# Windowed attention with a folded feed-forward on one core: another written order for steps 0 to 7, and five feed-forward slices between values and scores from step 8 on

## The chip, the cores and the metric

The kernel runs on one core of one Trainium2 chip. The metric is device time in microseconds (us). The engines are PE (TensorE), DVE (VectorE), ACT (ScalarE), POOL (GpSimd) and SP (SyncE), which here issues every transfer.

## The reference

Attention over 4 batches x 8 heads x 768 positions x 64, with a key kept if it is one of the first 8 or among the last 96, a bias that falls with distance, a softmax, and then a feed-forward part on all 3072 tokens:

```python
scores = scale * np.matmul(q, k.transpose(0, 1, 3, 2))
scores = np.where(keep, scores + bias[None, :, :, :], -1000000000.0)
scores = scores - np.max(scores, axis=-1, keepdims=True)
a = np.exp(scores)
a = a / (np.sum(a, axis=-1, keepdims=True) + 1e-09)
x = np.matmul(a, v)            # then 4 x 768 tokens of 512 numbers
a = x @ w1                     # w1, w2: 512 x 1024, float64
b = x @ w2
h = a * b @ w3                 # w3: 1024 x 1024, float64
return h @ w_out               # w_out: 1024 x 512, float64
```

## The kernel before, in words

**Attention** goes in 24 steps of 128 queries (all 8 heads, 6 steps to a batch). A step s has these parts, named as in the written order: `S.s`, the scores (64 small matmuls, L487); `R.s.q`, scores plus bias and their maxima, for four groups q of 32 queries (DVE, L496); `E.s.q`, the exponentials (ACT, L503); `s.s`, the sums and their reciprocals (DVE, L508 and L509); `c.s`, the scaling (ACT, L518, in steps 0 to 4, DVE, L521, after that); `X.s.0` and `X.s.1`, two transposes (DVE, L526); `V.s`, the values (128 small matmuls, 80 in the first step of a batch, L539); `h.s` and `l.s`, which copy the result out as a high and a low half (ACT L562, DVE L567). Scores and values go to one tile of PSUM, `sc`: in each of its four banks the values take the first 128 columns and the scores those behind. A step's keys and queries (`d.q<s>`) and values (`d.v<s>`) are loaded into two buffers each, so step s+2 loads what step s has left.

**The weights** come as float64 and are turned into float32 by DVE, in three instructions of 512 columns for each of 40 pieces: `A`, `B` and `C` (L143, L145, L147) of `t` (16 half blocks of w3), `o` (8 blocks of w_out) and `w` (16 blocks of w1 and w2). `d.x` loads a piece into one of eight landing buffers (L123), which is free again after the `C` of the piece before; w4 to w15 use only four of them. w3 and w_out are multiplied once: `F.f.k` is one of 64 fold matmuls (L167, each in two passes), `ph`/`pl` split the product, `wh`/`wl` split w1 and w2 (ACT and DVE).

**The feed-forward** goes in six units of 512 tokens, four steps each. A unit has 48 slices of six matmuls of 512 columns: 32 of the first product (`U.f.n.half`, L192 to L194) and 16 of the second (`Z.t.j`, L220 to L222). After the second slice of each f ACT copies out the gate `a` (L198), after the fourth DVE multiplies (`g`, L202), and `gh` and `gl` (L207, L212) split it.

**Order.** Steps 0 to 7, all weight work and unit 0 are issued from one hand-written list, `ORDER`: PE, DVE, ACT and SP each run their own part of it in that sequence. From step 8 on a loop sets the order of PE and ACT; DVE and SP follow a planner, which decides in advance by estimated times. Before the change a step's loop runs one slice after each of its four q groups, then half of `SLICES[s]`, then sums, scaling and transposes, the other half, the values, at once the scores of the next step, and only then `high(s)` and `low(s)`. `SLICES` is 4 for step 8 and 8 for the later ones.

Of the kernel before, what the change touches and what calls it, by code (L numbers as in the profile page):

```python
# [18 lines left out]
B, H, S, D = 4, 8, 768, 64  # L19
# [11 lines left out]
R = 32  # L31
# [5 lines left out]
NB = S // P  # L37
# [7 lines left out]
ORDER = """
d.t30 nt d.t00 d.q0 A.t30 B.t30 d.t20 bias d.o1 S.0 d.o0 A.t00 B.t00 C.t00 d.q2 C.t30 A.o1 B.o1 d.t41 A.o0 B.o0 d.t01 C.o0 C.o1 F.0.0 d.o2 A.t20 B.t20
d.o5 R.0.0 F.3.0 R.0.1 E.0.0 R.0.2 d.t31 E.0.1 R.0.3 A.t01 E.0.2 F.0.1 A.o2 d.v0 B.o2 E.0.3 F.3.1 d.t60 A.o5 B.t01 s.0 d.o4 C.t20 c.0 C.t01 F.2.0 d.o6
A.t31 B.o5 F.2.1 C.o2 d.t10 X.0.0 F.0.2 d.t11 X.0.1 F.3.2 A.o6 V.0 d.q1 B.o6 C.o6 F.2.2 A.t10 A.o4 d.o3 B.t10 h.0 l.0 C.t10 S.1 C.o5 B.t31 A.o3 F.1.0
d.q3 C.t31 R.1.0 F.1.1 R.1.1 E.1.0 R.1.2 F.1.2 E.1.1 R.1.3 B.o3 S.2 E.1.2 C.o3 E.1.3 B.o4 F.0.3 d.q4 s.1 C.o4 F.1.3 c.1 F.0.4 d.t51 F.3.3 d.t50 F.0.5
X.1.0 F.3.4 X.1.1 d.v1 A.t11 F.0.6 R.2.0 d.w4 F.3.5 R.2.1 E.2.0 A.t50 F.2.3 d.t21 E.2.1 B.t50 V.1 C.t50 d.v2 R.2.2 R.2.3 E.2.2 d.o7 A.t51 S.3 B.t11  # L50
E.2.3 C.t11 d.v3 h.1 F.3.6 l.1 d.w7 s.2 F.1.4 c.2 A.o7 B.o7 F.1.5 C.o7 F.1.6 B.t51 d.w14 F.0.7 X.2.0 F.1.7 d.t40 A.t21 ph.0 X.2.1 F.3.7 ph.1 pl.0 V.2
pl.1 ph.3 B.t21 C.t21 A.t40 F.2.4 d.t71 h.2 C.t51 l.2 F.5.0 d.w0 pl.3 F.2.5 B.t40 C.t40 F.5.1 A.t71 d.t70 F.2.6 B.t71 A.w0 F.5.2 C.t71 F.2.7 B.w0 d.w5
C.w0 F.5.3 ph.2 A.t70 d.w2 wh.0 F.4.0 pl.2 B.t70 F.5.4 C.t70 F.4.1 A.t41 d.w1 B.t41 F.7.0 C.t41 F.5.5 A.w2 B.w2 F.7.1 C.w2 F.5.6 A.w1 wh.2 F.7.2 B.w1
C.w1 F.5.7 wl.2 wh.1 F.7.3 R.3.0 ph.5 F.4.2 R.3.1 E.3.0 pl.5 F.7.4 E.3.1 R.3.2 F.4.3 R.3.3 E.3.2 wl.1 S.4 E.3.3 A.w5 B.w5 F.7.5 s.3 C.w5 c.3 F.4.4
A.t60 d.w11 B.t60 F.7.6 C.t60 d.w3 F.4.5 wl.0 wh.5 X.3.0 F.6.0 d.v4 X.3.1 F.7.7 d.t61 A.w4 F.6.1 ph.7 A.w3 V.3 B.w3 pl.7 C.w3 R.4.0 wh.3 F.6.2 A.t61
d.v5 E.4.0 wl.3 F.4.6 h.3 A.w7 l.3 F.6.3 B.w7 U.0.0.0 C.w7 B.t61 wh.7 d.w13 F.4.7 C.t61 U.0.0.1 R.4.1 ph.4 E.4.1 pl.4 F.6.4 wl.7 A.w11 U.0.1.0 R.4.2
R.4.3 E.4.2 F.6.5 B.w11 E.4.3 C.w11 U.0.1.1 s.4 wh.11 d.w6 B.w4 c.4 F.6.6 C.w4 U.1.0.0 wl.11 d.w8 wl.5 F.6.7 wh.4 X.4.0 U.1.0.1 ph.6 X.4.1 a.0 pl.6
V.4 a.1 g.0 A.w6 gh.0 B.w6 U.1.1.0 C.w6 gl.0 wh.6 d.w9 wl.6 U.1.1.1 wl.4 A.w8 U.2.0.0 g.1 A.w9 gh.1 B.w9 U.2.0.1 gl.1 B.w8 U.2.1.0 a.2 C.w8 C.w9 wh.8
d.w12 wh.9 U.2.1.1 wl.8 d.w15 wl.9 U.3.0.0 g.2 d.q6 A.w13 gh.2 A.w12 U.3.0.1 B.w12 d.q5 A.w15 C.w12 U.3.1.0 a.3 B.w15 d.w10 wh.12 C.w15 U.3.1.1 B.w13
wh.15 C.w13 S.5 g.3 wh.13 A.w10 gh.3 B.w10 U.4.0.0 C.w10 gl.2 wh.10 U.4.0.1 wl.10 A.w14 U.4.1.0 a.4 B.w14 C.w14 gl.3 wh.14 U.4.1.1 R.5.0 R.5.1 E.5.0  # L60
U.5.0.0 g.4 E.5.1 R.5.2 R.5.3 gh.4 U.5.0.1 E.5.2 gl.4 wl.13 S.6 E.5.3 wl.12 a.5 s.5 U.5.1.0 c.5 X.5.0 U.5.1.1 X.5.1 U.6.0.0 g.5 R.6.0 gh.5 R.6.1 E.6.0
U.6.0.1 gl.5 R.6.2 E.6.1 R.6.3 U.6.1.0 a.6 wl.15 E.6.2 wl.14 h.4 U.6.1.1 E.6.3 l.4 V.5 g.6 s.6 gh.6 c.6 U.7.0.0 h.5 d.v7 gl.6 l.5 X.6.0 d.v6 Z.0.0
d.q7 X.6.1 U.7.0.1 d.q8 Z.0.1 a.7 U.7.1.0 Z.0.2 U.7.1.1 V.6 g.7 gh.7 gl.7 S.7 h.6 Z.0.3 R.7.0 R.7.1 E.7.0 R.7.2 Z.1.0 ot.0 R.7.3 E.7.1 l.6 S.8 E.7.2
E.7.3 Z.1.1 s.7 c.7 Z.1.2 X.7.0 Z.1.3 X.7.1 V.7 ot.1 Z.2.0 h.7 l.7 Z.2.1 Z.2.2 Z.2.3 Z.3.0 ot.2 Z.3.1 Z.3.2 Z.3.3 ot.3
"""
W = 2 * T
SLOPES = [2.0 ** -(h + 1) for h in range(H)]
# [324 lines left out]
def banded(ctx, tc, ff, ns, nt, nf, oki, ident, qk, vx):  # L392
# [273 lines left out]
```

## Time and profile before

| what | value |
|---|---|
| median of 3 runs | 579.94 us (579.9 to 583.39) |
| the profiled execution | 583.23 us, its span 581.4 us |
| mean granted TensorE clock | 0.984 of full speed |
| PE busy | 534.8 us, 92% |
| DVE busy | 275.5 us, 47% |
| ACT busy | 196.5 us, 34% |

A busy PE is not PE at its peak, since matmuls are pipelined and the record of one covers parts of its neighbours. So what PE can lose is read from the distance of its starts, and from the stretches in which nothing starts. The profiled execution is 3.29 us longer than the median.

### The profile page before, as it was taken

What the parts mean: (1) busy time and instruction counts of PE and PEld (TensorE: products, weight loads), DVE (VectorE), ACT (ScalarE), POOL (GpSimd) and SP (SyncE); (2) the same over time, 40 slices, a digit from 0 to 9 for tenths busy, and PEclk for the clock granted to TensorE, in tenths of its full rate; (3) what the DMA queues carried; (4) which work ended last, traced back from release to release, by engine and by line L of the source; (5) the groups of instructions that cost most, each with busy time, mean ns of one, the idle gap of its engine ahead of it and who ended that gap; (6) DMA issues with size and microseconds to landing.
All of it is one profiled execution on the core that took longest, in us unless ns stands there. A gap on an engine that the chain in (4) does not pass through costs nothing.

```text
span 581.4 us, 14382 instructions
## 1 busy us (share of the span) xinstructions
PE 534.8 (92%) x6272; PEld 411.3 (71%) x6272; DVE 275.5 (47%) x779; ACT 196.5 (34%) x609; POOL 4.0 (1%) x26
## 2 busy tenths in 40 slices
PE   1776999989999999999999989999999999999995
PEld 0343445767778787788878778888877788888884
DVE  5874898989642445324534413544243454012200
ACT  4342334635432344323423331433234243122210
POOL 2000000000000000000000000000000000000000
PEclk9888899999999999999999989999999999999999
DMA  8958445361342112213220330222132000100011
GB/s 296 348 178 348 151 139 183 114 219 48 127 158 92 50 39 76 73 45 120 88 77 12 108 112 19 74 89 75 53 124 89 8 30 20 38 18 1 0 38 41
DMA packets 17879, 56.98 MB, mean 98 GB/s; under 512 B 1936, under 2 KB 3984, under 8 KB 17808
## 3 DMA queue, kind: packets, MB, share of 16 engines
q1 hardware_dynamic: 17808, 55.98, 27.7%
q8 instruction: 51, 0.84, 0.6%
q14 instruction: 20, 0.16, 0.1%
HBM read 49.68 MB, written 6.29 MB: 96 GB/s over the span
## 4 chain that ended last, share of the span: by engine, by line
PE 75%; DMA 10%; DVE 9%; issue 3%; ACT 1%; SPq 0%; ACTq 0%
PE m L192 13%; PE m L193 13%; PE m L194 13%; PE o L220 8%; PE o L221 7%; PE o L222 7%; PE sc L539 6%; PE sc L487 5%; PE w L167 2%; DMA stage<-w 2%; DMA raws<-w_out 2%; DMA more_raws<-w 1%; DMA qr<-qk 1%; DMA vr<-vx 1%; DVE t3s L147 1%
## 5 line engine op out<-in xcount | busy, mean ns | idle before, releaser
L503 ACT ACTIVATE pr<-pr,mx 128x136 f32<-128x136 f32 (+2 forms) x192 | 74.5, 390 | 31.7 <-DVE mx L496 31.7
L202 DVE TENSOR_TENSOR g<-m,a 128x512 f32<-128x512 f32 x48 | 33.1, 689 | 101.6 <-PE m L194 101.2
L192 PE MATMUL m<-xh,w1h 128*128 128x512 f32 x192 | 77.3, 402 | 0.4 <-ACT xh L562 0.4
L220 PE MATMUL o<-wh,gh 128*128 128x512 f32 x192 | 76.7, 400 | 0.0
L192 PE MATMUL m<-xh,w2h 128*128 128x512 f32 x192 | 75.7, 394 | 0.0
L221 PE MATMUL o<-wl,gh 128*128 128x512 f32 x192 | 75.5, 393 | 0.0
L222 PE MATMUL o<-wh,gl 128*128 128x512 f32 x192 | 75.3, 392 | 0.0
L193 PE MATMUL m<-xl,w1h 128*128 128x512 f32 x192 | 75.0, 391 | 0.2 <-DVE xl L567 0.2
L194 PE MATMUL m<-xh,w1l 128*128 128x512 f32 x192 | 74.8, 390 | 0.0
L194 PE MATMUL m<-xh,w2l 128*128 128x512 f32 x192 | 74.7, 389 | 0.0
L193 PE MATMUL m<-xl,w2h 128*128 128x512 f32 x192 | 74.7, 389 | 0.0
L167 PE MATMUL w<-wo,t 128*128 128x512 f32 x128 | 64.9, 655 | 7.3 <-DVE wo L147 4.3
L207 ACT ACTIVATE gh<-g 128x512 fp32r<-128x512 f32 x48 | 30.3, 631 | 115.5 <-DVE g L202 115.5
L487 PE MATMUL sc<-qr 64*32 64x136 f32 (+3 forms) x1536 | 33.3, 288 | 30.7 <-DMA qr<-qk 14.9
L567 DVE TENSOR_TENSOR xl<-sc,xh 128x512 fp32r<-128x512 f32 x24 | 16.6, 691 | 82.6 <-ACT xh L562 82.5
L167 PEld LDWEIGHTS w<-wo,t 128*128 128x128 f32 x128 | 26.0, 211 | 38.6 <-issue 26.4
L487 PEld LDWEIGHTS sc<-qr 64*32 64x32 f32 x1536 | 23.1, 111 | 37.9 <-issue 16.6
L539 PEld LDWEIGHTS sc<-pt,vr 32*64 32x64 f32 x2880 | 38.5, 130 | 11.9 <-issue 6.7
L198 ACT ACTIVATE a<-m 128x512 f32<-128x512 f32 x48 | 28.5, 594 | 51.4 <-PE m L194 51.2
L212 DVE TENSOR_TENSOR gl<-g,gh 128x512 fp32r<-128x512 f32 x48 | 33.1, 690 | 22.6 <-ACT gh L207 22.3
L192 PEld LDWEIGHTS m<-xh,w1h 128*128 128x128 f32 x192 | 36.0, 188 | 11.0 <-issue 2.4
L220 PEld LDWEIGHTS o<-wh,gh 128*128 128x128 f32 x192 | 36.4, 189 | 9.3 <-issue 1.9
(85 smaller groups left out, 619.1 us busy)
## 6 DMA issues: line engine op xcount, KB each, us to landing
qr<-qk SPq DMA_DIRECT2D x20, 720.0 KB, 5.6
vr<-vx SPq DMA_DIRECT2D x20, 512.0 KB, 4.0
out_dram<-ot SPq DMA_DIRECT2D x24, 256.0 KB, 2.0
stage<-w3t SPq DMA_DIRECT2D x9, 512.0 KB, 5.2
raws<-w SPq DMA_DIRECT2D x6, 512.0 KB, 4.0
more_raws<-w SPq DMA_DIRECT2D x6, 512.0 KB, 3.6
more_raws<-w_out SPq DMA_DIRECT2D x5, 512.0 KB, 8.5
qr<-qk SPq DMA_DIRECT2D x4, 528.0 KB, 5.3
```

The costliest lines, as they stand in the source:

```text
L167: self.nc.tensor.matmul(self.prod[f], lhsT=self.t3[f, z][:, i * P:(i + 1) * P].bitcast(F32), rhs=self.wo[:, k].bitcast(F32), start=k == 0, ...
L192: self.nc.tensor.matmul(ps, lhsT=mh, rhs=xh[:, i], start=i == 0, stop=False)
L193: self.nc.tensor.matmul(ps, lhsT=mh, rhs=xl[:, i], start=False, stop=False)
L194: self.nc.tensor.matmul(ps, lhsT=ml, rhs=xh[:, i], start=False, stop=i == NCC - 1)
L202: self.nc.vector.tensor_tensor(out=self.g[f], in0=self.ps[f, 1], in1=self.a[f], op=ALU.mult)
L212: self.nc.vector.tensor_tensor(out=self.gl[:, f], in0=self.g[f], in1=self.gh[:, f].bitcast(F32), op=ALU.subtract)
L220: self.nc.tensor.matmul(ps, lhsT=self.gh[:, f, ts], rhs=ff.wh[:, f], start=f == 0, stop=False)
L221: self.nc.tensor.matmul(ps, lhsT=self.gh[:, f, ts], rhs=ff.wl[:, f], start=False, stop=False)
L222: self.nc.tensor.matmul(ps, lhsT=self.gl[:, f, ts], rhs=ff.wh[:, f], start=False, stop=f == NFC - 1)
L487: nc.tensor.matmul(sc[hp * R:(hp + 1) * R, i, cols], lhsT=m[rows, hp, KW + q * R:KW + (q + 1) * R], rhs=m[rows, hp, k0 + w0:k0 + w1], star ...
L503: nc.scalar.activation(x, x, AF.Exp, bias=mx[:, q, u:u + 1], scale=-1.0, accum_out=sm[:, q, u:u + 1])
L539: nc.tensor.matmul(sc[cols, hp, q0 * R:q1 * R], lhsT=v[rows, i, cols], rhs=pt[rows, u, i, q0 * R:q1 * R], start=n == 0, stop=n == len(bloc ...
```

## The change

`SLICES` goes. In the loop from step 8 on the split is fixed: one slice after each q group, none before the sums, three between the transposes and the values, then `high(s)` and `low(s)`, then five slices, then the scores of the next step. A step has 12 slices in both kernels, but step 8, which had 8 and now has 12.

`ORDER` is replaced by another sequence of the same 504 entries. The size check is now loaded first, followed by w3's blocks t10, t11 and t31 and by w_out's o1, o4, o2 and o3; the first fold is of row 1; scores and values stand mostly apart from each other on PE; w15 is loaded early and unpacked last of all.

```diff
-SLICES = [4] * 9 + [8] * (B * NB - 9)
 ORDER = """
-d.t30 nt d.t00 d.q0 A.t30 B.t30 d.t20 bias d.o1 S.0 d.o0 A.t00 B.t00 C.t00 d.q2 C.t30 A.o1 B.o1 d.t41 A.o0 B.o0 d.t01 C.o0 C.o1 F.0.0 d.o2 A.t20 B.t20
...
+nt d.t10 d.t11 d.t31 bias d.o1 A.t10 B.t10 d.o4 A.t11 C.t10 d.o2 B.t11 C.t11 d.o3 A.t31 A.o1 B.t31 d.q0 C.t31 A.o4 d.o0 B.o1 A.o2 B.o2 d.t20 C.o1 C.o2
+d.q1 A.o3 S.0 B.o3 C.o3 d.t00 A.o0 B.o0 d.t30 C.o0 R.0.0 F.1.0 d.q2 R.0.1 E.0.0 R.0.2 E.0.1 F.1.1 R.0.3 A.t20 E.0.2 S.1 d.v0 A.t00 B.t00 E.0.3 d.o6
+C.t00 F.1.2 s.0 d.t50 A.t30 c.0 F.0.0 B.t30 F.1.3 d.t01 B.t20 C.t20 F.0.1 d.v1 C.t30 F.2.0 X.0.0 F.0.2 d.q3 X.0.1 F.3.0 A.o6 B.o6 V.0 d.w15 A.t01 C.o6
+R.1.0 d.o5 F.0.3 R.1.1 E.1.0 R.1.2 F.3.1 d.t70 h.0 R.1.3 E.1.1 F.2.1 B.t01 E.1.2 S.2 C.t01 l.0 E.1.3 B.o4 F.3.2 d.q4 s.1 A.o5 c.1 F.2.2 B.o5 C.o4
+F.3.3 d.o7 C.o5 F.1.4 d.t71 X.1.0 F.0.4 X.1.1 F.1.5 d.t41 R.2.0 V.1 R.2.1 E.2.0 d.w2 R.2.2 E.2.1 A.o7 B.o7 F.1.6 h.1 C.o7 E.2.2 F.0.5 l.1 R.2.3 F.1.7
+E.2.3 S.3 A.w2 ph.1 B.w2 F.0.6 C.w2 d.q5 s.2 wh.2 pl.1 F.3.4 c.2 A.t50 F.0.7 d.t60 B.t50 F.3.5 C.t50 d.t21 wl.2 F.2.3 ph.0 X.2.0 F.3.6 d.t40 pl.0
+F.5.0 X.2.1 d.v2 F.3.7 R.3.0 R.3.1 E.3.0 F.5.1 R.3.2 ph.3 A.t21 F.5.2 E.3.1 B.t21 F.5.3 C.t21 E.3.2 A.t40 F.2.4 R.3.3 A.t70 E.3.3 S.4 A.t41 B.t41
+C.t41 V.2 d.q6 s.3 B.t40 c.3 d.t51 C.t40 F.2.5 A.t60 B.t60 d.w4 F.4.0 B.t70 h.2 F.2.6 X.3.0 F.4.1 X.3.1 F.2.7 l.2 A.t51 F.4.2 ph.2 A.t71 pl.3 F.4.3
...
+X.4.1 U.0.0.0 ph.4 R.5.0 pl.4 E.5.0 V.4 R.5.1 R.5.2 E.5.1 R.5.3 E.5.2 wl.4 S.6 C.t61 E.5.3 wl.5 U.0.0.1 s.5 A.w9 B.w9 F.6.4 C.w9 U.0.1.0 c.5 wh.9 d.w7
...
+U.2.1.1 C.w8 B.w10 wh.8 d.w11 U.3.0.0 g.2 C.w10 gh.2 wh.10 d.w14 U.3.0.1 gl.2 wl.10 wl.8 U.3.1.0 a.3 A.w12 B.w12 U.3.1.1 C.w12 A.w14 wh.12 d.w13 B.w14
+U.4.0.0 g.3 C.w14 gh.3 U.4.0.1 A.w11 wh.14 gl.3 wl.12 U.4.1.0 a.4 A.w13 B.w11 C.w11 U.4.1.1 B.w13 wh.11 C.w13 U.5.0.0 g.4 wh.13 gh.4 wl.13 U.5.0.1
+gl.4 wl.11 a.5 U.5.1.0 A.w15 B.w15 C.w15 U.5.1.1 wl.14 wh.15 wl.15 U.6.0.0 g.5 h.4 gh.5 l.4 U.6.0.1 gl.5 V.5 a.6 U.6.1.0 X.6.0 h.5 d.v7 l.5 d.q8 X.6.1
+Z.0.0 R.7.0 R.7.1 E.7.0 U.6.1.1 R.7.2 E.7.1 R.7.3 Z.0.1 g.6 E.7.2 U.7.0.0 gh.6 E.7.3 gl.6 S.8 s.7 c.7 Z.0.2 U.7.0.1 V.6 a.7 U.7.1.0 X.7.0 h.6 l.6
+U.7.1.1 X.7.1 V.7 g.7 gh.7 gl.7 Z.0.3 h.7 l.7 Z.1.0 ot.0 Z.1.1 Z.1.2 Z.1.3 Z.2.0 ot.1 Z.2.1 Z.2.2 Z.2.3 Z.3.0 ot.2 Z.3.1 Z.3.2 Z.3.3 ot.3
 """
...
                     slices(1)
-                slices(SLICES[s] // 2)
                 sums(s)
                 scale(s, nc.vector)
                 turn(s, 0)
                 turn(s, 1)
-                slices(SLICES[s] - SLICES[s] // 2)
+                slices(3)
                 values(s)
+                high(s)
+                low(s)
+                slices(5)
                 if s + 1 < n:
                     scores(s + 1)
-                high(s)
-                low(s)
             slices(10 ** 6)
```

## Rows read from the trace of the kernel before

**Rows 1.** The page, its first part: busy time, share of the span and instructions of PE and DVE.

```profile
PE 534.8 (92%) x6272; PEld 411.3 (71%) x6272; DVE 275.5 (47%) x779; ACT 196.5 (34%) x609; POOL 4.0 (1%) x26
```

**Rows 2.** Busy time by stretches: the stretch, its length, each engine's busy time and instructions, the granted clock, the DMA engines' share, GB/s.

```profile
0.00:62.00 62.00, 38.05 (x513) 19.20 (x514) 40.52 (x119) 25.13 (x91) 3.97 (x26) 0.89 0.74 275
62.00:99.00 37.00, 35.64 (x390) 16.89 (x389) 32.11 (x74) 13.97 (x41) 0.00 (x0) 1.00 0.54 184
99.00:151.00 52.00, 47.72 (x434) 36.43 (x434) 46.40 (x115) 27.01 (x80) 0.00 (x0) 1.00 0.31 107
...
187.00:504.00 317.00, 306.55 (x4038) 251.00 (x4036) 129.60 (x399) 106.27 (x343) 0.00 (x0) 0.99 0.20 65
```

**Rows 3.** The instructions of PE in order of time around the end of the written order (start, duration, engine, line, tiles, shape).

```profile
186.32 0.39 PE L192 MATMUL m<-xh,w1h 128*128 128x512 f32 x1
```

**Rows 4.** All that PE waited for from 187 to 505 us: total, times, longest.

```profile
PE sc L487 <- issue: 10.4, 9, 1.6
```

**Rows 5.** PE in order of time from the last slice before V.9 to the first after S.10; in brackets the idle time before an instruction and what ended it.

```profile
217.73 0.39 PE L194 MATMUL m<-xh,w2l 128*128 128x512 f32 x1
218.05 1.81 PE L539 MATMUL sc<-pt,vr 32*64 32x128 f32 x128
219.79 0.69 PE L487 MATMUL sc<-qr 64*32 64x136 f32 x31
221.81 0.74 PE L487 MATMUL sc<-qr 64*32 64x136 f32 x33 [1.33 <-issue]
222.47 0.50 PE L192 MATMUL m<-xh,w1h 128*128 128x512 f32 x1
222.82 0.40 PE L193 MATMUL m<-xl,w1h 128*128 128x512 f32 x1
```

**Rows 6.** The page, its third part: the queue that carries instructions (packets, MB, share).

```profile
q8 instruction: 51, 0.84, 0.6%
```

**Rows 7.** The chain of waits from step 8 to step 23: start, length, what. V.8, the gap in S.16 and a slice behind it, V.16 with S.17 and V.17, and V.23.

```profile
197.36 1.74 PE sc L539 x87
...
341.90 1.60 issue
...
345.03 0.43 PE o L221
...
362.52 1.74 PE sc L539 x88
364.26 1.13 PE sc L487 x64
...
381.94 1.74 PE sc L539 x87
...
502.38 1.74 PE sc L539 x88
```

**Rows 8.** Busy time by stretches, the one behind the gap in S.16 (columns as in rows 2).

```profile
344.00:347.00 3.00, 3.00 (x27) 2.21 (x11) 1.94 (x14) 1.60 (x6) 0.00 (x0) 0.57 0.61 178
```

**Rows 9.** DVE in order of time in step 10, from the product of its fourth slice to its transposes.

```profile
228.29 0.69 DVE L202 TENSOR_TENSOR g<-m,a 128x512 f32<-128x512 f32 x1 [0.17 <-PE m L194]
...
229.12 1.29 DVE L521 TENSOR_TENSOR pr<-pr,sm 128x1088 f32<-128x1088 f32 x1
230.33 0.69 DVE L212 TENSOR_TENSOR gl<-g,gh 128x512 fp32r<-128x512 f32 x1
230.94 1.56 DVE L526 STREAM_TRANSPOSE pt<-pr 128x640 f32<-128x640 f32 x2
```

**Rows 10.** ACT in order of time in step 10: the gate that stands between the second and the third of its four groups of exponentials.

```profile
225.77 0.58 ACT L198 ACTIVATE a<-m 128x512 f32<-128x512 f32 x1
```

**Rows 11.** The chain of waits from 95 to 152 us: the pace of one matmul of a slice and of one fold (two passes).

```profile
100.56 0.23 PE m L192
...
101.25 0.86 PE w L167 x2
```

**Rows 12.** Groups of DVE instructions by line in 0 to 200 us (count, busy time, mean ns of one, idle time before): the first and the third instruction of an unpacking.

```profile
L147 DVE SCALAR_TENSOR_TENSOR t<-stage,t 128x512 int32<-128x512 int32 x9 | 6.2, 689 | 0.2
...
L143 DVE TENSOR_SCALAR t<-stage 128x512 int32<-128x512 int32 x9 | 3.8, 424 | 1.0 <-DMA stage<-w3t 1.0
```

**Rows 13.** The loads of weight pieces (L123) in 0 to 187 us: who waited for their landing (us, times), and the time from issue to landing.

```profile
  DVE t L143: 8.3, 5
  DVE t3s L143: 5.2, 8
  DVE wo L143: 4.8, 4
...
DMA to landing us min/median/max: 3.4/5.1/12.7
```

**Rows 14.** SP in order of time: the issue of q3 and q4, after 6.5 us in which SP issued nothing.

```profile
36.39 4.69 SPq L458 DMA_DIRECT2D qr<-qk  x2
```

**Rows 15.** Busy time by stretches, 10 to 15 us (columns as in rows 2).

```profile
10.00:15.00 5.00, 0.99 (x43) 0.50 (x31) 3.22 (x6) 4.84 (x15) 0.25 (x2) 1.00 1.02 408
```

**Rows 16.** PE in order of time in the first 62 us: S.0, the first folds, and the second part of S.3.

```profile
9.51 1.48 PE L487 MATMUL sc<-qr 64*32 64x40 f32 x64 [9.51 <-DMA qr<-qk]
15.24 6.13 PE L167 MATMUL w<-wo,t 128*128 128x512 f32 x8 [4.26 <-DVE wo L147]
...
56.15 1.15 PE L487 MATMUL sc<-qr 64*32 64x136 f32 x29 [3.30 <-issue]
```

More of the change, by code (lines that the diff above doesn't have):

```diff
@@ L43 @@
 FIRST = 5
-SLICES = [4] * 9 + [8] * (B * NB - 9)
 ORDER = """
-d.t30 nt d.t00 d.q0 A.t30 B.t30 d.t20 bias d.o1 S.0 d.o0 A.t00 B.t00 C.t00 d.q2 C.t30 A.o1 B.o1 d.t41 A.o0 B.o0 d.t01 C.o0 C.o1 F.0.0 d.o2 A.t20 B.t20
-d.o5 R.0.0 F.3.0 R.0.1 E.0.0 R.0.2 d.t31 E.0.1 R.0.3 A.t01 E.0.2 F.0.1 A.o2 d.v0 B.o2 E.0.3 F.3.1 d.t60 A.o5 B.t01 s.0 d.o4 C.t20 c.0 C.t01 F.2.0 d.o6
-A.t31 B.o5 F.2.1 C.o2 d.t10 X.0.0 F.0.2 d.t11 X.0.1 F.3.2 A.o6 V.0 d.q1 B.o6 C.o6 F.2.2 A.t10 A.o4 d.o3 B.t10 h.0 l.0 C.t10 S.1 C.o5 B.t31 A.o3 F.1.0
@@ L49 @@
[L49 to L64, printed above, removed]
+nt d.t10 d.t11 d.t31 bias d.o1 A.t10 B.t10 d.o4 A.t11 C.t10 d.o2 B.t11 C.t11 d.o3 A.t31 A.o1 B.t31 d.q0 C.t31 A.o4 d.o0 B.o1 A.o2 B.o2 d.t20 C.o1 C.o2
@@ new lines @@
+E.2.3 S.3 A.w2 ph.1 B.w2 F.0.6 C.w2 d.q5 s.2 wh.2 pl.1 F.3.4 c.2 A.t50 F.0.7 d.t60 B.t50 F.3.5 C.t50 d.t21 wl.2 F.2.3 ph.0 X.2.0 F.3.6 d.t40 pl.0
+F.5.0 X.2.1 d.v2 F.3.7 R.3.0 R.3.1 E.3.0 F.5.1 R.3.2 ph.3 A.t21 F.5.2 E.3.1 B.t21 F.5.3 C.t21 E.3.2 A.t40 F.2.4 R.3.3 A.t70 E.3.3 S.4 A.t41 B.t41
+C.t41 V.2 d.q6 s.3 B.t40 c.3 d.t51 C.t40 F.2.5 A.t60 B.t60 d.w4 F.4.0 B.t70 h.2 F.2.6 X.3.0 F.4.1 X.3.1 F.2.7 l.2 A.t51 F.4.2 ph.2 A.t71 pl.3 F.4.3
+pl.2 C.t70 F.4.4 R.4.0 d.w10 F.7.0 R.4.1 E.4.0 R.4.2 F.4.5 d.w0 E.4.1 R.4.3 F.7.1 B.t71 E.4.2 d.w1 C.t71 S.5 E.4.3 B.t51 d.v4 C.t51 F.7.2 s.4 d.q7
@@ new lines @@
+C.t60 c.4 F.5.4 A.w0 F.6.0 B.w0 d.w5 C.w0 F.7.3 A.w1 wh.0 F.6.1 B.w1 d.w3 F.7.4 C.w1 wl.0 d.t61 wh.1 F.6.2 A.w4 wl.1 F.7.5 d.v3 B.w4 F.6.3 A.w5 B.w5
+F.7.6 C.w4 F.5.5 C.w5 wh.4 d.w9 F.7.7 wh.5 A.t61 A.w3 F.5.6 d.w12 ph.7 B.w3 pl.7 V.3 C.w3 B.t61 wh.3 wl.3 F.5.7 h.3 X.4.0 F.4.6 l.3 ph.5 pl.5 F.4.7
+X.4.1 U.0.0.0 ph.4 R.5.0 pl.4 E.5.0 V.4 R.5.1 R.5.2 E.5.1 R.5.3 E.5.2 wl.4 S.6 C.t61 E.5.3 wl.5 U.0.0.1 s.5 A.w9 B.w9 F.6.4 C.w9 U.0.1.0 c.5 wh.9 d.w7
+F.6.5 X.5.0 U.0.1.1 X.5.1 R.6.0 F.6.6 R.6.1 E.6.0 A.w7 U.1.0.0 E.6.1 B.w7 C.w7 F.6.7 R.6.2 wh.7 d.w6 U.1.0.1 R.6.3 a.0 wl.9 ph.6 d.v6 g.0 E.6.2 S.7
@@ new lines @@
+pl.6 gh.0 wl.7 a.1 U.1.1.0 gl.0 E.6.3 A.w6 s.6 U.1.1.1 B.w6 C.w6 wh.6 d.w8 U.2.0.0 g.1 c.6 gh.1 d.v5 U.2.0.1 gl.1 wl.6 U.2.1.0 a.2 A.w10 A.w8 B.w8
+U.2.1.1 C.w8 B.w10 wh.8 d.w11 U.3.0.0 g.2 C.w10 gh.2 wh.10 d.w14 U.3.0.1 gl.2 wl.10 wl.8 U.3.1.0 a.3 A.w12 B.w12 U.3.1.1 C.w12 A.w14 wh.12 d.w13 B.w14
+U.4.0.0 g.3 C.w14 gh.3 U.4.0.1 A.w11 wh.14 gl.3 wl.12 U.4.1.0 a.4 A.w13 B.w11 C.w11 U.4.1.1 B.w13 wh.11 C.w13 U.5.0.0 g.4 wh.13 gh.4 wl.13 U.5.0.1
+gl.4 wl.11 a.5 U.5.1.0 A.w15 B.w15 C.w15 U.5.1.1 wl.14 wh.15 wl.15 U.6.0.0 g.5 h.4 gh.5 l.4 U.6.0.1 gl.5 V.5 a.6 U.6.1.0 X.6.0 h.5 d.v7 l.5 d.q8 X.6.1
```

## Prediction

> **What bounds the kernel now.** The page's first part is read first, and not believed: PE is busy for 92% of the span [rows 1], but a busy PE may start nothing, so the stretches come next [rows 2]. The written order ends where unit 1's first matmul starts, at 186.3 us [rows 3]; of the 40.1 us that PE isn't busy before 504 us, 10.45 lie behind 187 us, and most of the rest before 62 us, where the granted clock is also lower, 0.89 [rows 2]. So there are two cases.
>
> From 187 us to 504 us PE waited only for "issue", 10.4 us in 9 pieces, all inside scores [rows 4]. The order of time shows one: V.9 runs without a pause, 31 matmuls of S.10 follow, then PE waits 1.33 us for nothing that the profile shows, and goes on [rows 5]. V and S stand together in this loop: 192 matmuls, each with its weight load. Instructions come in packets of 16 KB, 51 for 0.84 MB [rows 6], and PE's 2 x 6272 instructions [rows 1] are 12,544: if a packet holds 256, that is 49 packets. A step has 264 matmuls, two packets and some more, so a packet's edge would wander slowly through the steps, which the place of the gap does (31 matmuls into S here). I read the gap as V and S eating a packet faster than the next one comes.
>
> In the written order PE has 143.3 us of work: 64 folds at 0.86, 48 slices of six at 0.227 [rows 11], nine S at 1.13, six V at 1.74 [rows 7] and two short ones, estimated from their 80 of 128 matmuls at 1.2. It ends at 186.3, so 43 us are lost. DVE has 142 us of work there, counted in the same way (an unpacking is 0.42 and twice 0.69 [rows 12]), and is the second bound: from 62 to 151 us it is busy for 78.5 of 89 us [rows 2]. Its largest loss is the landing of weight pieces, 18.3 us in 17 waits, the first piece's 4.6 included [rows 13].
>
> **The loop from step 8.** *What goes.* V.16 to V.17 is a step without a gap, 19.42 us; V.8 to V.23 is 305.0 us [rows 7]. Two of the 15 steps start with a short V (estimated 0.55 less), two have a short S (estimated 0.2 less): without gaps they would take 289.8. So the gaps cost 15.2 us: the 10.4 themselves, a slower rest of S behind them, and once the clock. After the longest gap, 1.60 us, the slices go at 0.43 a matmul instead of 0.23 [rows 7], with a granted clock of 0.57 over that stretch, the lower of its two levels for most of it [rows 8]: about 1.9 us.
>
> With 30 slice matmuls between V and S no run of small matmuls is longer than 128. From V's 31st matmul, where a packet would end 128 before the gap, to where S went on is 221.81 + 0.03 - 218.5 = 3.3 us; call that a packet's time to come. V lasts 1.8, so a packet that holds V and six slice matmuls (1.4) or more lasts long enough. Only an edge within six matmuls of V's start still costs, up to 1.3: 12 places of 132, so one or two steps of 16. I take 1.0 us back, bounds 0 and 6 (if four steps meet it, since the place wanders slowly).
>
> *What is added.* One more change from slices to small matmuls and back in each step. In [rows 5] a slice's last start to V is 0.32 instead of 0.23, and S's end to the second slice matmul is 0.35 where 0.23 would do: 0.2 to 0.3, 16 times, 4.0 us.
>
> *What moves: the values come sooner.* V(s) now stands 7 slices behind S(s), not 12: 9.72 us after S's end instead of 16.52 (S.10 ends at 222.55; 5 x 1.36 less). The chain between them is maxima, exponentials, sums, scaling, transposes; in step 10 it ended at 232.50 [rows 9], 9.95 us after S. That is too late by 0.2, were it unchanged. Two things change. `high` and `low` no longer lie between S and the maxima, but this gives little in a step of the first product: ACT's third group of exponentials stands behind the gate of the second slice (225.77 [rows 10]), which PE sets. And `gl` of the fourth slice, which took 0.61 ahead of the transposes [rows 9], comes after them in the program; the planner may keep it there or not. So X ends 9.35 to 9.95 after S, V waits 0 to 0.35 with its semaphore, in the 12 steps of 16 that have a gate there; in the others the chain has no gate and is 1.7 shorter. I take 1.0 us in all, bounds 0 and 4.2. What is queued behind V on PE are its own five slices and the next scores, so a wait of V is lost in full.
>
> *What costs nothing.* `high` and `low` (0.6 and 0.69) lie beside five slices, 6.8 us; without that cover S(s+1) would wait for both, 1.5 us. SP: step s+2's values and keys wait as before for V(s) and S(s), and have a step to land. Step 8 has four slices more and the rest behind V.23 fewer, at the same pace.
>
> Sum for the loop: -15.2 + 4.0 + 1.0 + 1.0 = -9.2 us.
>
> **The written order.** The same 504 entries, so the work of each engine is unchanged, and only its losses count.
>
> *Landing waits.* For each piece I summed DVE's work between the `C` that frees its buffer and its own `A`, from the two lists with the durations of [rows 12]. A landing takes at least 3.4 us and 5.1 at the median [rows 13]. Before, eleven pieces have 4.4 us of cover or less (o6, o3, t71, w0, t70, w2, w1, w9, w12, w15, w10: 3.2 to 4.4). After, five (w7, w6, w8, w14, w13: 3.7 to 4.4); all others that reuse a buffer have 6.7 or more. Before, SP also stood for 6.5 us in front of q3, which waited for S.1 [rows 14]; in the new order S.1 stands third on PE, q3 finds its buffer free, and only q4 and q5 can hold SP up, in front of pieces with 9 us of cover or more.
>
> *The start.* Folding begins later: q0 is the eighth piece and o0 the ninth, and DVE does 15.1 us of work (the bias, seven unpackings and part of an eighth) before the first fold can start, so it starts at about 20.4 instead of 15.24 [rows 16]. But then t10, t11, t31 and four w_out blocks lie ready. Followed by hand down the lists, with a transfer every 1.28 us (512 KB at the 408 GB/s that full queues move [rows 15]), S.3 ends at 51 us (57.3 before, with a gap of 3.30 [rows 16]), and V.2 at 65 us with 38.7 us of PE's work done. DVE's idle time by 62 us is then 10.6 us; it was 21.5 [rows 2].
>
> *Then DVE sets the pace.* w11 is its tightest piece: 125.6 us of DVE's work stand before it is split, and 41.2 us of PE's work behind that. Idle time: 10.6, plus 1.4 where R.5.1 waits for V.4 (both touch `sc`, and V.4 stands between R.5.0 and R.5.1), 1.0 of landings, 0.5 at the gates: 13.5. 125.6 + 13.5 + 41.2 = 180.3; with 1.7 for changes between shapes and for the wait of Z.0.3 on the last `gl` it ends at 182.0, 4.3 us earlier. S.4 with V.2 and V.4 with S.6 still stand together, 192 matmuls; a gap there (3.30 at the worst) is hidden as long as DVE is behind PE. Bounds: 177 (half of DVE's idle time gone) to 190 (one more wait like q3's, and a gap that DVE waits out).
>
> **Sum.** The profiled execution's own time is 583.2; -9.2 - 4.3 gives 569.7. The median of the runs is 3.3 us lower; from it the sum would give 566.4. Which losses the faster executions lack isn't shown; if they are some of the gaps, these can't be saved twice. I take 568.
>
> **The rivals.**
> (a) *The gaps are not a packet's.* For the packets: two fetches' worth of instructions in a step, and the wandering place. Against: nothing names the releaser. Then the gaps stay in S, the added changes of shape cost 4.0, and only the written order gains: 579.9 - 4.3 + 4.0 = 580. The Trainium skill says this too: "Runtime: NRT & Kernel Launch", section "Instruction fetch mechanics", has crossing a block cost one tail-bump, mostly hidden, as dispatch is slower than the fill. By that rule the gaps would be something else; rows 5 speak against it, but don't name the cause.
> (b) *V's wait takes the gaps' place*, the one that ends slower. The place is X in front of V. It decides from 0.9 us a step (13.5 over 15 steps). If the planner puts the next gate's product or `low` ahead of the transposes, X ends 1.5 to 2 later, 1.8 x 12 = 21 us: 589. Against it: no other DVE work is ready before 9.7 us after S.
> (c) *The written order loses.* SP stands in front of q5 until a late S.3, t21 and t40 land late, and DVE, which has no slack left, ends 10 us later: 578.
> (d) *It gains more*: 177 us and no edge at V's start: 562.
>
> **How the numbers follow.** Forecast 0.62 (562 to 574), (a) 0.10, (b) 0.06, (c) 0.12, (d) 0.10. The range 559 to 579 leaves out (b), half of (a) and the tails. About 1% is what a measurement of this kernel can tell from none. Below 574.1 lie nearly all of the forecast, (d) and a little of (c): 0.72; within 1% (a), most of (c), a little of the forecast: 0.21; above 585.7 (b) and a tail: 0.07.
>
> **What would show it.** Right: no "issue" in scores from step 9 on, or one or two at V's start; V 9.7 us after S, X ending before it; unit 1's first matmul near 182; S.3's end near 51. Wrong in the loop: the nine gaps still there, or PE waiting for L526. Wrong in the order: DVE's waits for landings above 10 us before 151, or PE short of folds before 60.

## The result, and the profile after

The changed kernel takes 562.58 us at the median against 580.27 for the kernel before in the same session: ratio 0.968 [0.964, 0.972], 3.2% faster. In a second session it was 562.58 against 579.79, 0.969 [0.966, 0.972]. The forecast was 568, with a range from 559 to 579. One execution of the changed kernel, the profiled one of the first session, took 884.02 us with a granted clock of 0.57, and another 605.02 with 0.855; both are left out of the ratios, and the profile after is that of the same kernel in the second session (563.24 us, span 561.4). Line numbers after the change are one lower than before (scores L486, values L538, slices L191 to L193 and L219 to L221).

The page's first part, to be read against [rows 1]:

```profile
PE 526.8 (94%) x6272; PEld 405.1 (72%) x6272; DVE 273.9 (49%) x779; ACT 197.4 (35%) x609; POOL 4.0 (1%) x26
```

PE's busy time fell by 8.0 us with the same 6272 matmuls. The stretches tell more (columns as in [rows 2]):

```profile
0.00:62.00 62.00, 40.82 (x595) 19.80 (x595) 48.82 (x147) 30.53 (x111) 3.96 (x26) 1.00 0.79 295
62.00:99.00 37.00, 33.02 (x577) 17.80 (x572) 32.12 (x84) 17.88 (x59) 0.00 (x0) 1.00 0.58 207
99.00:151.00 52.00, 48.90 (x429) 38.25 (x429) 45.45 (x103) 22.30 (x60) 0.00 (x0) 1.00 0.36 116
...
187.00:504.00 317.00, 317.00 (x4090) 257.71 (x4089) 128.76 (x399) 107.73 (x339) 0.00 (x0) 1.00 0.20 66
```

From 187 to 504 us PE is busy without a pause where it had lost 10.45 us, and starts 52 matmuls more. By 62 us DVE has done 48.8 us of work, 8.3 more than before. The granted clock of that stretch is 1.00 instead of 0.89.

All that PE waited for in the whole run (total, times, longest), to be read against [rows 4]:

```profile
PE sc L486 <- DMA qr<-qk: 16.8, 2, 15.4
PE w L166 <- DVE t L146: 3.9, 2, 2.5
PE w L166 <- DVE wo L146: 3.3, 3, 1.8
PE m L193 <- DVE w2l L159: 1.6, 1, 1.6
PE sc L486 <- DVE mx L495: 1.5, 1, 1.5
PE sc L538 <- DMA vr<-vx: 0.8, 1, 0.8
PE sc L486 <- issue: 0.2, 1, 0.2
```

The nine "issue" waits are gone; one of 0.2 us is left, in S.6 of the written order. Nothing here is a wait of values for their transposes (L525). Unit 1's first matmul, the end of the written order, starts at 178.12 us (186.32 in [rows 3]):

```profile
178.12 0.39 PE L191 MATMUL m<-xh,w1h 128*128 128x512 f32 x1
```

From there to PE's last matmul it is 377.0 us, where it was 388.7. So of the 20.0 us between the two profiled executions, 8.2 lie ahead of unit 1's first matmul and 11.8 behind it (388.75 less 376.97). In the texts below "T1" is that start and "the rest" is what follows it.

### The profile page after: what moved, and what is told of

The parts are those of the page before. It is cut to its first block, busy times and chain, and to the rows that moved or that the text cites. A ratio compares the mean times of both kernels' runs of the same rounds, so it can differ in the third digit from the quotient of the medians.

```text
span 882.2 us, 14384 instructions
## 1 busy us (share of the span) xinstructions
PE 857.3 (97%) x6272; PEld 477.3 (54%) x6272; DVE 275.9 (31%) x779; ACT 197.8 (22%) x609; POOL 4.0 (0%) x26
## 3 DMA queue, kind: packets, MB, share of 16 engines
q1 hardware_dynamic: 17808, 55.98, 18.1%
## 5 line engine op out<-in xcount | busy, mean ns | idle before, releaser
L191 PE MATMUL m<-xh,w1h 128*128 128x512 f32 x192 | 112.0, 584 | 0.0
L191 PE MATMUL m<-xh,w2h 128*128 128x512 f32 x192 | 111.9, 583 | 0.0
L192 PE MATMUL m<-xl,w1h 128*128 128x512 f32 x192 | 111.3, 580 | 0.0
L221 PE MATMUL o<-wh,gl 128*128 128x512 f32 x192 | 110.6, 576 | 0.0
L193 PE MATMUL m<-xh,w1l 128*128 128x512 f32 x192 | 110.5, 575 | 0.0
L193 PE MATMUL m<-xh,w2l 128*128 128x512 f32 x192 | 110.3, 575 | 0.0
L219 PE MATMUL o<-wh,gh 128*128 128x512 f32 x192 | 110.3, 575 | 0.0
L166 PE MATMUL w<-wo,t 128*128 128x512 f32 x128 | 101.1, 968 | 1.8 <-DVE wo L146 1.8
L191 PEld LDWEIGHTS m<-xh,w1h 128*128 128x128 f32 x192 | 42.1, 219 | 36.4 <-issue 22.9
L495 DVE CUSTOM_DVE_ANT_0 pr<-sc,biasw 128x136 f32<-128x136 f32 x160 | 36.9, 294 | 75.0 <-PE sc L486 59.8
L192 PEld LDWEIGHTS m<-xl,w1h 128*128 128x128 f32 x192 | 42.7, 222 | 30.6 <-issue 17.7
L219 PEld LDWEIGHTS o<-wh,gh 128*128 128x128 f32 x192 | 41.6, 217 | 32.2 <-issue 19.8
L538 PEld LDWEIGHTS sc<-pt,vr 32*64 32x64 f32 x2880 | 48.8, 141 | 18.9 <-issue 18.4
L192 PEld LDWEIGHTS m<-xl,w2h 128*128 128x128 f32 x192 | 41.9, 218 | 31.2 <-issue 20.7
L221 PEld LDWEIGHTS o<-wh,gl 128*128 128x128 f32 x192 | 42.6, 222 | 30.0 <-issue 17.0
```

Source lines behind the costliest of these rows:

```text
L166: self.nc.tensor.matmul(self.prod[f], lhsT=self.t3[f, z][:, i * P:(i + 1) * P].bitcast(F32), rhs=self.wo[:, k].bitcast(F32), start=k == 0, ...
L191: self.nc.tensor.matmul(ps, lhsT=mh, rhs=xh[:, i], start=i == 0, stop=False)
L192: self.nc.tensor.matmul(ps, lhsT=mh, rhs=xl[:, i], start=False, stop=False)
L193: self.nc.tensor.matmul(ps, lhsT=ml, rhs=xh[:, i], start=False, stop=i == NCC - 1)
L219: self.nc.tensor.matmul(ps, lhsT=self.gh[:, f, ts], rhs=ff.wh[:, f], start=f == 0, stop=False)
L221: self.nc.tensor.matmul(ps, lhsT=self.gl[:, f, ts], rhs=ff.wh[:, f], start=False, stop=f == NFC - 1)
```

## The experiments

Two theories stood against each other in the loop: a *packet of instructions* that comes too late for 192 small matmuls in a row, and a gap that belongs to *the scores themselves* (their buffer, their keys, the engine). In the written order the question was what the 8.2 us were made of.

**The changed kernel again**, on the chip of the next three, so that there is a trace to compare.

> The changed kernel once more, for a profile with the full clock (the first one shows a granted clock of 0.56 nearly throughout). Expected 562 us, 18 under the kernel before. If the reasons of the prediction hold: no idle time inside scores from step 9 on, V 9.7 us after the end of S, unit 1's first matmul near 182 us. Since 18 us were gained and 13.5 forecast, either the written order ends near 178, or the loop lost less than the 6 us that were set against its 15.2.

Measured: the profile above. V.10 with the slices on both sides, and S.10 ahead of it, in PE's order of time (to be read against [rows 5]):

```profile
215.84 0.39 PE L193 MATMUL m<-xh,w2l 128*128 128x512 f32 x1
216.16 1.20 PE L486 MATMUL sc<-qr 64*32 64x136 f32 x64
217.28 0.50 PE L191 MATMUL m<-xh,w1h 128*128 128x512 f32 x1
...
227.03 1.81 PE L538 MATMUL sc<-pt,vr 32*64 32x128 f32 x128
228.76 0.50 PE L191 MATMUL m<-xh,w2h 128*128 128x512 f32 x1
...
235.79 1.20 PE L486 MATMUL sc<-qr 64*32 64x136 f32 x64
```

S and V each run in one piece, and from S.10 to S.11 it is 19.63 us, the length that a step without a gap had before (19.42 in [rows 7]) plus 0.21.

**The two halves alone.** One kernel has the new `ORDER` and the old loop, another the old `ORDER` and the new loop.

```diff
 # order only: before, with
-ORDER = """ (old) """
+ORDER = """ (new) """
 # loop only: before, with the loop's lines of the change
-                slices(SLICES[s] // 2)
...
+                slices(3)
                 values(s)
+                high(s)
+                low(s)
+                slices(5)
```

> The new written order with the loop as it was. Theory 1 (terms as forecast): the order is worth 4.3 us, so 576. Theory 2 (the order is what was undersized): it is worth about 8.5, so 571 to 572. In both the gaps of about 1.1 us inside scores stay from step 9 on, at other places, since the packets' edges fall elsewhere.

> The old written order with the new loop. Theory 1: the loop is worth 9.2 us, so 571. Theory 2 (the loop was undersized, its shape changes and waits of V cost nearly nothing): about 13.5 to 15, so 565 to 567. If the gaps have nothing to do with packets of instructions: no gain, 580 to 584.

Measured: the order alone 576.25, ratio 0.992 [0.989, 0.995]; the loop alone 569.19, ratio 0.983 [0.980, 0.986]. What PE waited for behind 180 us in the order-only kernel:

```profile
PE sc L487 <- issue: 11.2, 9, 2.0
```

The loop-only kernel has no wait of PE at all there. Its T1 is 182.7 and its rest 377.0; the order-only kernel has 178.7 and 389.5. So each half does its own part and nothing to the other's stretch. The order's time is what its first theory had (576); the loop's lies between its two (571, and 565 to 567). In times the halves give 4.6 [2.8, 6.4] and 10.1 [8.3, 11.9] us, 14.7 together, where the whole gives 18.1 [16.4, 19.8]. The difference of 3.4 is about as much as these intervals leave open; whether any of it is real isn't settled.

**One slice between.** In the kernel before, one slice of six matmuls moves from before the values to between values and scores; `high` and `low` stay behind the scores.

```diff
-                slices(SLICES[s] - SLICES[s] // 2)
+                slices(SLICES[s] - SLICES[s] // 2 - 1)
                 values(s)
+                slices(1)
                 if s + 1 < n:
                     scores(s + 1)
```

> The kernel before, with one of the slices ahead of the values moved behind them, so that one slice (six matmuls, 1.36 us) stands between values and the next scores; everything else, the late copies included, as before. Packets of 256 instructions that take 3.3 us to come: V's 1.8 us and one slice's 1.4 make 3.2, so the gaps shrink to 0.2 us or less each and nearly all of the loop's gain is here, 568 to 572. Rival: the gain of the changed loop comes from the early copies or from five slices of distance, and one slice does little: 577 to 581, gaps of 0.8 us and more in scores.

Measured: 570.63, ratio 0.984 [0.981, 0.987], rest 377.5, and PE waits for nothing from 187 to 505 us. In order of time, V.13, the slice and S.14:

```profile
291.86 1.80 PE L539 MATMUL sc<-pt,vr 32*64 32x128 f32 x128
293.59 0.50 PE L192 MATMUL m<-xh,w2h 128*128 128x512 f32 x1
...
295.18 1.37 PE L487 MATMUL sc<-qr 64*32 64x136 f32 x64
```

This is one of five steps in which S lasts longer than its 1.20 us (1.23 to 1.42): all that is left of the gap. Six matmuls, 1.4 us, do nearly what the change's 30 do (rest 377.0), and the order of the copies plays no part.

**Scores ahead of values.** The run of 192 stays, but the two change places.

```diff
-                values(s)
                 if s + 1 < n:
                     scores(s + 1)
+                values(s)
```

> The kernel before, with the next scores put directly ahead of the values in the loop instead of directly behind them. The run of 192 small matmuls is as long as before. Packets of instructions: the gaps stay, 1.0 to 1.7 us each in most steps, but stand in the values now (L539), 128 matmuls behind an edge that lies in the scores or just ahead of them; time 578 to 582. Rival: the gaps belong to the scores, their tile or their semaphores: then they stay in L487, or go, and with them 10 us or more (566 to 571).

Measured: 576.94, ratio 0.996 [0.993, 0.999], 1 us under the range expected. What PE waited for from 187 to 505 us, and one place in order of time:

```profile
PE sc L539 <- issue: 9.1, 9, 1.3
```

```profile
215.44 1.20 PE L487 MATMUL sc<-qr 64*32 64x136 f32 x64
216.56 1.48 PE L539 MATMUL sc<-pt,vr 32*64 32x128 f32 x95
219.23 0.50 PE L539 MATMUL sc<-pt,vr 32*64 32x96 f32 x33 [1.19 <-issue]
```

The gap now stands in the *values*, whichever comes second, and the scores are whole. It belongs to the length of the run, so it is not the scores' buffer or keys. Here the gap comes 95 matmuls into V. An edge 128 matmuls before that is the 32nd of S, at about 215.98 (31 of 64 in 1.12 us); V goes on at 219.23, some 3.25 us later. The same working gave 3.3 us from [rows 5]. In the trace itself, where each matmul has its start, the distance is 2.8 to 3.4 us in the nine gaps here and 2.9 to 3.7 in the nine of the kernel before.

**Half a slice between.** Three matmuls between values and scores, the other three behind the scores.

```diff
-                slices(SLICES[s] - SLICES[s] // 2)
+                slices(SLICES[s] - SLICES[s] // 2 - 1)
                 values(s)
+                half()        # three of the next slice's six matmuls
                 if s + 1 < n:
                     scores(s + 1)
+                half()        # the other three
```

> The kernel before, with half a slice (three matmuls, 0.7 us) of the 12 between values and scores, the other half behind the scores. Packets: the run of one packet is 0.7 us longer, so each gap of 1.0 to 1.6 us shrinks by about 0.7, to 0.3 to 0.9; V-to-V 20.3 where it was 21.0 and 19.8 with a whole slice; time about 575. Rival: any work of another shape between the two breaks what makes the gap: no gap at all, 570.

Measured: 576.23, ratio 0.995 [0.992, 0.997], rest 383.6. What PE waited for from 187 to 505 us (the scores are line 492 in this kernel):

```profile
PE sc L492 <- issue: 3.2, 7, 0.7
```

With 0, 3, 6 and 30 matmuls between, the longest gap is 1.6 [rows 4], 0.7, none and none: three matmuls last 0.7 us and shorten it by about that.

**The packets themselves.** The traces also hold the time of each of the 51 instruction packets of [rows 6], and they settle what the experiments leave to argument. In the kernel before, one packet of 16 KB is transferred from 219.59 to 220.47 us, and S.10 [rows 5] goes on at 221.81, 1.34 us behind the transfer's end. It is so at every gap that the four kernels with gaps have behind 187 us (nine before, nine with the order alone, nine with scores first, seven with half a slice): PE goes on 1.19 to 1.56 us after the end of a packet's transfer, and this transfer begins 0.5 to 1.2 us after the start of the matmul that stands 128 ahead. Packets come 3 to 19 us apart there, so this is no chance. The two longest gaps, 1.60 us before and 2.0 with the order alone, have transfers of 1.43 and 1.71 us, where the shortest take 0.88. The trace doesn't name the engine that a packet is for.

The place of the gap says that the packet is PE's and what it holds. Count PE's instructions in the trace from its first one (matmuls, weight loads and the waits of its sequencer): in all four kernels the first matmul behind each of the 34 gaps is the 192nd or 193rd behind a multiple of 256. So these pauses stand at the edges of blocks of 256 instructions, and since a step has 264 matmuls, two blocks and some more, an edge comes 8 or 9 matmuls sooner in each step: before the change the gap stands 40, 31 and 23 matmuls into S in steps 9 to 11.

**One slice more behind the values**, to price rival (b): the values come 1.4 us sooner than in the change.

```diff
-                slices(3)
+                slices(2)
                 values(s)
                 high(s)
                 low(s)
-                slices(5)
+                slices(6)
```

> The changed kernel with the values one slice sooner: 6 slices between scores and values, 6 between values and scores. In the 12 steps with a gate X ended 0.62 to 0.74 us ahead of V's start, and a slice is 1.36: V should wait 0.7 us in each of them, 8.5 to 9 us in all, 571. If the planner's order of DVE changes with it, X can end up to 0.6 sooner and the wait is near zero: 563.

Measured: 568.72, ratio 0.979 [0.975, 0.984]. The rest is 385.6 us, 8.6 more than the change's; the medians, of two sessions, are only 6.1 apart. The rest is the better measure, since it is 377.0 in both profiles above that have the change's loop. What PE waited for behind 180 us, and one such place:

```profile
PE sc L538 <- DVE pt L525: 3.5, 12, 0.3
```

```profile
205.36 0.43 PE L538 MATMUL sc<-pt,vr 32*64 32x128 f32 x2
206.09 1.79 PE L538 MATMUL sc<-pt,vr 32*64 32x128 f32 x126 [0.30 <-DVE pt L525]
```

Twelve waits, one in each step with a gate behind its second slice, as foretold. The row shows 0.30 us, but V's third matmul starts 0.73 after its first: a wait costs what the starts show, not what stands in brackets. A step is 20.40 here and some 19.65 in the change, and 12 times 0.75 is 9.0.

**Five loads moved** in the changed order, to price rival (c). The trace after shows SP standing in front of a load that waits for S or V, with other loads behind it. SP's issues in order of time, and the piece of w3 that came late for it, on DVE:

```profile
47.73 0.33 SPq L457 DMA_DIRECT2D qr<-qk  x1
48.15 1.36 SPq L122 DMA_DIRECT2D stage<-w3t  x1
49.61 0.37 SPq L122 DMA_DIRECT2D more_raws<-w3t  x1
```

```profile
57.88 0.43 DVE L142 TENSOR_SCALAR t<-more_raws 128x512 int32<-128x512 int32 x1 [3.06 <-DMA more_raws<-w3t]
```

`q5` waits until S.3 has ended, at 47.73, and t21 and t40 are issued behind it. The experiment moves `d.q5`, `d.q6`, `d.w10`, `d.v3` and `d.q8` behind loads that are free to go.

```diff
-C.w2 d.q5 s.2 ... X.2.1 d.v2 F.3.7
+C.w2 s.2 ... X.2.1 d.v2 d.q5 F.3.7
-V.2 d.q6 s.3 ... B.t60 d.w4 F.4.0
+V.2 s.3 ... B.t60 d.w4 d.q6 F.4.0
-R.4.0 d.w10 F.7.0 ... d.w1 C.t71 ... F.7.5 d.v3 B.w4
+R.4.0 F.7.0 ... d.w1 d.w10 d.v3 C.t71 ... F.7.5 B.w4
-d.w13 B.w14 ... d.v7 l.5 d.q8 X.6.1
+d.w13 d.q8 B.w14 ... d.v7 l.5 X.6.1
```

> The changed kernel with five loads moved in SP's order alone: q5 behind v2, q6 behind w4, w10 behind w1, v3 ahead of q7, q8 ahead of v7. In the changed kernel SP stands in front of q5 until S.3 ends and of q6 until S.4 ends, and DVE then waits 3.06 us for t21, 1.58 for t51 and 1.24 for w0; PE waits 1.46 for q8 and 0.83 for v3. If DVE's idle time sets the end of the written order: unit 1 starts 4 to 6 us sooner than 178.1, and the time is 557 to 559. If another engine is as late there: under 1.5 us.

Measured: 556.41, ratio 0.959 [0.956, 0.963], 6.2 us below the change and a little more than expected. Who waited for the landing of a weight piece (us, times), first in the changed kernel, then here, to be read against [rows 13]:

```profile
  DVE t L142: 6.4, 5
  DVE t3s L142: 2.0, 3
```

```profile
  DVE t L143: 2.0, 3
  DVE t3s L143: 0.6, 1
```

The landing waits fall from 8.4 to 2.6 us, and T1 falls by 6.8:

```profile
171.28 0.39 PE L192 MATMUL m<-xh,w1h 128*128 128x512 f32 x1
```

Of those 6.8 us, 5.3 lie ahead of the split of w11, the last split that PE waits for (1.6 us in the changed kernel, 1.7 here): it ends at 129.50 where it ended at 134.83, and DVE has been idle for 15.4 us by then instead of 20.4. The other 1.5 lie behind it: PE no longer waits 1.46 us for q8, which is a wait for a load and not for DVE.

**A sooner first fold**, on top of that: o0 changes places with o4, so that the fold of row 1 doesn't wait for the ninth piece.

```diff
-B.t10 d.o4 A.t11 ... A.o4 d.o0 B.o1 ... d.t00 A.o0 B.o0 d.t30 C.o0 R.0.0
+B.t10 d.o0 A.t11 ... A.o0 d.o4 B.o1 ... C.o1 B.o0 C.o0 ... d.t00 A.o4 d.t30 R.0.0
```

> The kernel with the five loads moved (556.4 us), and in it w_out's block o0 loaded and unpacked in the place of o4, so that the first fold can start 1.5 to 2 us sooner than 18.6 us. If DVE's work and idle time set the end of the written order, the sooner start of PE is worth nothing: unit 1 starts within 0.5 us of 171.3, time 556 to 557. If PE's own late start is what is lost: 1.5 to 2 us sooner in both.

Measured: 557.14, ratio 0.960 [0.956, 0.963]. The first fold starts 1.8 us sooner than the change's 18.60, and unit 1 no sooner than without it:

```profile
16.76 3.62 PE L167 MATMUL w<-wo,t 128*128 128x512 f32 x4
```

```profile
171.71 0.39 PE L192 MATMUL m<-xh,w1h 128*128 128x512 f32 x1
```

With the first fold 1.8 us sooner T1 would have to be near 169.5 if PE's start set it; it is 171.7. T1 varies by up to 2 us between executions with the same order (176.7 to 178.7 for the changed one), so this speaks against PE's start and doesn't prove it alone.

**w11 split sooner**, on top of the five loads: `wl.11` stands right behind `g.4`.

```diff
-B.w13 wh.11 C.w13 U.5.0.0 g.4 wh.13 gh.4 wl.13 U.5.0.1 gl.4 wl.11 a.5
+B.w13 wh.11 C.w13 U.5.0.0 g.4 wl.11 wh.13 gh.4 wl.13 U.5.0.1 gl.4 a.5
```

> The kernel with the five loads moved, and in it the low half of w11 split right behind g.4, ahead of the low half of w13 and of gl.4 (two DVE instructions, 1.37 us, sooner). PE waits 1.7 us for it in the run before. If w11 is the last piece on DVE that holds PE up: unit 1 starts 1.0 to 1.7 us sooner than 171.3, and the time, which can hardly show it, is 555. If what comes behind it (V.5 to V.7, the last gl) is as late: no change.

Measured: 555.94, ratio 0.958 [0.955, 0.961], the fastest kernel of this study, though not apart from the one with five loads moved. PE's wait for that half of w11, there and here, and T1:

```profile
PE m L194 <- DVE w2l L160: 1.7, 1, 1.7
```

```profile
PE m L194 <- DVE w2l L160: 0.5, 1, 0.5
```

```profile
170.44 0.39 PE L192 MATMUL m<-xh,w1h 128*128 128x512 f32 x1
```

The wait shrinks by 1.2 and T1 by 0.84 (1.0 to 1.7 expected), which is less than T1 varies. That DVE sets the end of the written order rests mainly on the five loads: 5.8 us less of DVE's waiting for landings, w11's split 5.3 sooner, and PE waiting for it as before. The two kernels after that agree with it, but their steps are too small to add much.

## Why the prediction was right, and where its terms were off

The direction, the cause and both halves came as forecast; the sum was 569.7 on the profiled execution, and it came out 563.2. The 6.5 us too few are 2.6 in the loop and 3.9 in the order.

**The loop: -11.8 instead of -9.2.** The term of -15.2 for the gaps stands, by its two observations (the run of 192, and no gap in V or S alone), by the experiments with 0, 3, 6 and 30 matmuls and by the packets' times. Three smaller terms were mis-sized.
- *Changes of shape*: 4.0 was foretold, 0.25 a step. A step is 19.63 to 19.67 where it was 19.42, so 0.23 in 15 steps, 3.4.
- *An edge at V's start*: 1.0 foretold, nothing measured. No V and no S waits for "issue" behind 187 us. This is luck in part: counted in blocks of 256 as above, only one edge falls within six matmuls of a V's start, the place that the forecast feared, and it is 5 matmuls into V.18, one of the short ones of 80.
- *V waits for X*: 1.0 foretold, nothing measured. V stands 9.68 to 9.71 us after S's end (9.72 foretold). DVE in step 10, to be read against [rows 9]:

```profile
223.03 1.29 DVE L520 TENSOR_TENSOR pr<-pr,sm 128x1088 f32<-128x1088 f32 x1
224.25 0.68 DVE L201 TENSOR_TENSOR g<-m,a 128x512 f32<-128x512 f32 x1
224.85 1.56 DVE L525 STREAM_TRANSPOSE pt<-pr 128x640 f32<-128x640 f32 x2
226.33 0.65 DVE L211 TENSOR_TENSOR gl<-g,gh 128x512 fp32r<-128x512 f32 x1
```

`gl`, which might have gone on standing ahead of the transposes, comes behind them, and X ends 8.95 to 9.09 after S where 9.35 to 9.95 was foretold; V is spared by 0.6 us. In the four steps without a gate X ends 7.03 to 7.10 after S. With these three terms as measured, -15.2 + 3.4 is -11.8, which is what the two profiles differ by.

**The written order: -8.2 on the profiled executions instead of -4.3.** T1 varies from one execution to the next: the five profiles with the old order have 186.3, 182.7, 184.7, 183.9 and 185.7, mean 184.7; the three with the new one 178.1, 178.7 and 176.7, mean 177.8. By these the order gives 6.8, and 1.6 of the 8.2 is that the profile of before was a late one; by times the order-only kernel gives 4.6 [2.8, 6.4].
- *The walk by hand held*: R.5.1 waits for V.4 1.29 us (1.4 foretold), S.6 waits 1.50 for the maxima in front of it, S.3 ends at 47.7 (51), V.2 at 63.8 (65).
- *The start was put too late*: the first fold starts at 18.60, not 20.4. The forecast's 20.4 less its 15.1 us of work has DVE start at 5.3; it starts at 3.85, when the size check has landed. By the experiment with o0 a sooner first fold alone is worth nothing; whether DVE's sooner start is worth its 1.45 us was not tried alone.
- *DVE's work and its idle time were both mis-sized, against each other*: up to the split of w11 125.6 us of work and 13.5 of idle time were foretold, 139.1 together. w11's split ends at 134.83 (the row below: 134.14 and 0.69), 4.3 sooner. By then DVE is busy for 114.4 us and idle for 20.4. The forecast went by the durations of single instructions, but the records of neighbours overlap: those of this stretch add up to 132.0 us and cover 114.4. So the order ends sooner than foretold because the work is shorter than it was counted, and not because DVE waits less; by 62 us too it has been idle for 13.2 us (62 less 48.8), where 10.6 was foretold. What PE has left behind the split came out right, 43.3 us to T1 with 42.9 foretold, but 1.46 of it is a wait for q8 that no term had.

```profile
134.14 0.69 DVE L159 TENSOR_TENSOR w2l<-t3s,w2h 128x512 fp32r<-128x512 f32 x1
```

- *Two gaps of 192* (S.4 with V.2, V.4 with S.6) cost 0 and 0.20 us. V.4 and S.6 are held apart by S.6's wait for the maxima:

```profile
94.43 1.80 PE L538 MATMUL sc<-pt,vr 32*64 32x128 f32 x128
97.74 0.29 PE L486 MATMUL sc<-qr 64*32 64x40 f32 x12 [1.50 <-DVE mx L495]
98.23 0.87 PE L486 MATMUL sc<-qr 64*32 64x40 f32 x52 [0.20 <-issue]
```

**The rivals.** (a) *Not a packet's*: it falls by the experiments with scores first, half a slice and one slice, and by the packets' times. The Trainium skill ("Runtime: NRT & Kernel Launch", section "Instruction fetch mechanics") has the fetch mostly hidden, since dispatch is slower than the fill; on this point the measurement differs, 10.4 us in nine pieces that shrink with what stands between, and at each of them the trace has a packet that lands 1.2 to 1.6 us before PE goes on. (b) *V's wait*: real, and 0.6 us away; one slice more behind V costs 8.6 us of the rest. (c) *The written order loses*: its mechanism was there, exactly where it was put, t21 behind q5, with 3.06 us of waiting. It was too small to turn the sign; with the four other loads it is the 6.2 us that the change left lying. The prediction had said that q4 and q5 hold up only pieces with 9 us of cover: that step failed, since a load that is issued late on SP has its cover used up before it starts. (d) named 177 and no edge: 562, and is nearer to what came than the forecast is.

**Open** are what passes in the 1.2 to 1.6 us between a packet's landing and PE's going on, and why the two halves' times add up to 3.4 us less than the whole. In the traces they do add up: the order's T1 of 178.7 and the loop's rest of 377.0 make 555.7, and the whole has 178.1 + 377.0 = 555.1.

## What to carry to other kernels

Where PE pauses for nothing that the profile names, count the small matmuls in a row up to the pause; if the pause wanders and moves with the run, put a few long matmuls into the run, here one slice of 1.4 us for every 192, and first make sure that what then comes sooner, here the values, still finds its input ready. In a written order, look on the queue that issues loads for one that waits for a buffer, and for what stands behind it: moving five loads was worth 6.2 us here. And find which engine ends the order last before making another one start sooner.

## What the runs showed of the hardware that was not expected

A pause of PE can be followed by some 3.4 us at the lower of the two granted levels, as in [rows 8], or not, and its length alone doesn't decide. In the order-only kernel S.6 waits 1.50 us, and behind it matmuls of a slice go at 0.43 instead of 0.23 until 101.8 us (in order of time, then the stretch with its granted clock in columns as in [rows 2]):

```profile
98.38 1.61 PE L487 MATMUL sc<-qr 64*32 64x40 f32 x64 [1.50 <-DVE mx L496]
...
100.50 0.63 PE L193 MATMUL m<-xl,w1h 128*128 128x512 f32 x1
100.93 0.63 PE L194 MATMUL m<-xh,w1l 128*128 128x512 f32 x1
```

```profile
98.00:103.00 5.00, 4.62 (x73) 3.39 (x73) 4.90 (x13) 2.35 (x11) 0.00 (x0) 0.66 0.01 3
```

The same wait of 1.50 us at the same place of the same order, in the changed kernel (the rows of S.6 above), was followed by slices at full speed; there the granted clock is at its full level from 21.8 us to the end of the matmuls. In the order-only kernel the gap of 2.0 us at 415.8 was followed by such a stretch as well, the gaps of 1.3 us were not. So a gap costs more than its own length. Measured from one V to the next, against the 19.42 us of a step without a gap, it costs 0.3 to 0.4 us more where the clock stays, and about 1.9 more where it falls (22.97 us for the step of S.16 before, 23.38 for the one with 2.0 us). What decides whether it falls was not tried.
